# Talking-heads attention and a gated MLP in one kernel: more buffers for scores, and operand differences of the fast matrix products spread over their runs

## The chip, the core and the metric

One core of a Trainium2 chip. The metric is the device time of one launch in microseconds (us), here as the median of three runs. The engines are named as the profile names them: PE (TensorE, matmuls), PEld (its weight loads), DVE (VectorE), ACT (ScalarE), POOL (GpSimd) and SP (SyncE, which issues every DMA of this kernel on one queue).

## The reference, cut to what matters

```
scores = scale * q @ k^T                      # (4 batches, 12 heads, 448, 448)
scores = einsum('bhij,hg->bgij', scores, w_pre)
attn   = exp(scores - max);  attn /= sum + 1e-9
attn   = einsum('bhij,hg->bgij', attn, w_post)
x      = (attn @ v) as (1792 tokens, 768)
h      = x @ w_in                             # w_in 768 x 2048, float64 in memory
out    = (h * sigmoid(h)) @ w_out             # w_out 2048 x 768, float64 in memory
```

## The kernel before, in words

**Attention.** Each of 4 batches is cut into 4 tiles of 110 or 120 query rows; a tile is 11 or 12 groups of ten rows times twelve heads (120 partitions), 180 groups in all. The loop over `groups` writes out one order for all engines. In iteration i, PE mixes group i+3 over the heads (`mix`, L318), DVE takes its maximum (`top`, L324), ACT its exponential (`exp`, L329), POOL scales the second mixing weights by the row sums (`norm`, L337, tile `wr`), and PE mixes group i again (`mix_again`, L344). In between stand pieces of work that `put` has spread over the groups: `scores` (L265) multiplies q and k of the next tile for two heads, ACT copies the two results to `st` tiles (L283), and SP moves each into the grouped layout `g` (L284); `values` (L287) multiplies the mixed weights with v, ACT and DVE bring the two halves together in `xb`, and after every second head SP stores `xb` to `x_dram` (L306). The `st` tiles rotate through 3 buffers of pool `s`, the `wr` tiles through 3.

**Weights.** `convert` turns the MLP's float64 weights into float32 in jobs of two parts, a part in three steps: DVE L86, ACT L90, DVE L92 and L93, then in `finish` DVE L63 and POOL L66. After a job's second part POOL makes sums of the four quarter blocks (L68 to L71), and SP stores seven planes to DRAM (L57). 34 of the 48 jobs run inside attention, the other 14 beside the first matrix product.

**MLP.** Both matrix products are done by a fast scheme with seven multiplications instead of eight on 2 x 2 blocks. The tokens fall into two units u of two batches each. I call one pass of a multiplication for both units a run. The first matrix product (kind "i") has 7 runs of 16 products (products 0 to 111 of list `steps`), each product being 9 matmuls; the second (kind "o") has 7 runs of 6 products (112 to 153) of 24 matmuls. Each float32 operand is split in two float32r halves: `halve` is an ACT cast (L537) and a DVE subtraction (L539). A run's operands are either blocks of x (or of the activated hidden values) or differences of blocks: `differ` (DVE L543, POOL L545) and `second` (DVE L550, ACT L552, POOL L553, DVE L555). `put_at` spreads such items over the products ahead of the run that needs them. In each product of the main loop the order is: matmuls, `ready_part` (ACT cast L520 and POOL subtraction L521 of 256 KB of weights, tiles `wh` and `wl`, `WB` = 7 buffers each), `load_part` (L515), `evacuate` of the product before (DVE or ACT), `put_out` for finished outputs (PE transposes L756, ACT L757, SP L758), then the operand items, then one chunk of `load_x` (SP L481, POOL L476) and one step of `convert`. Product results rotate through four PSUM banks. Unit 0's x is loaded inside attention through two buffers `xr`; unit 1's after attention, one chunk per product.

Of the kernel before, what the change touches and what calls it, by code (L numbers as in the profile page):

```python
# [37 lines left out]
def convert(nc, pool, ebias, jobs):  # L38
# [15 lines left out]
    def store():  # L54
        while made:
            dst, g = made.pop(0)
            nc.sync.dma_start(out=dst, in_=g)  # L57

    def finish(k, pair, g, e):
        n, i = parts[k]  # L60
        lo, hi = pair[:, :, :, 0], pair[:, :, :, 1]
        m = lo.bitcast(F32)
        nc.vector.scalar_tensor_tensor(  # L63
            out=m, in0=lo.bitcast(U32), scalar=(1 if i else -1) * 2.0 ** -32, in1=hi,
            op0=ALU.mult, op1=ALU.add if i else ALU.subtract)
        nc.gpsimd.tensor_mul(out=e, in0=m, in1=e)  # L66
        if not i:
            nc.gpsimd.tensor_add(out=g[:, 4], in0=g[:, 0], in1=g[:, 1])  # L68
            nc.gpsimd.tensor_add(
                out=g[:, 5:7], in0=g[:, 0:5:4], in1=g[:, 2:3].to_broadcast([128, 2, 128]))  # L70
            nc.gpsimd.tensor_add(out=g[:, 0], in0=g[:, 6], in1=g[:, 3])  # L71
            made.append((jobs[n][1], g))

    before = None
    for k in range(len(parts)):
# [4 lines left out]
        if k % 2 == 0:  # L80
            g = pool.tile([128, 7, 128], F32, name="cg", tag="cg", bufs=2)
# [22 lines left out]
def talking_heads_then_silu_mlp(  # L104
# [16 lines left out]
    R = 10  # L121
# [41 lines left out]
    s_p = pool("s", 3, late, side="right")  # L163
# [18 lines left out]
    def load_weights():  # L182

        wrep = e_p.tile([GP, 2, H], F32, name="wrep", tag="wr", bufs=3)
# [3 lines left out]
        blk = e_p.tile([GP, R], F32, name="blk", tag="wr", bufs=3)  # L188
# [98 lines left out]
    def values(n, h):  # L287
# [8 lines left out]
        if h % 2 == 0:  # L296
            xbs[n] = s_p.tile([128, 2, TQ], F32, name="xb", tag="xb" if n + 1 < len(seq) or h % 4 else "s", bufs=2 if n + 1 < len(seq) or h % 4 else 3)
# [5 lines left out]
        def add():  # L303
            nc.vector.tensor_add(out=xb[:, h % 2, :m], in0=po[:, m:2 * m], in1=xb[:, h % 2, :m])  # L304
            if h % 2:
                nc.sync.dma_start(  # L306
                    out=x_dram[b].rearrange("(h p) t -> p h t", p=128)[:, h - 1:h + 1, t0:t0 + m], in_=xb[:, :, :m])
        return [(take, add)]

    class Group:  # L310
# [21 lines left out]
        def norm(self):  # L332
# [3 lines left out]
            self.wr = e_p.tile([GP, GP], F32, name="wr", tag="wr", bufs=3)  # L336
# [22 lines left out]
    kns, vns, qns, ks, vs, qs, gs, ats, xbs = {}, {}, {}, {}, {}, {}, {}, {}, {}  # L359
    jobs = [(wi_src[:, f, c], wi_dram[:, :, f * HC + c, :]) for f in range(HF) for c in range(HC)]  # L360
# [105 lines left out]
    ORDER = (2, 3, 6, 5, 1, 4, 0)  # L466
# [3 lines left out]
    def load_x(u, blocks, lag):  # L470

        chunks = [(j, l, c) for j, l in blocks for c in range(HC)]
        for n in range(len(chunks) + lag):
            if n >= lag:
                r = box["xr"][(n - lag) % 2]
                nc.gpsimd.tensor_add(out=xs[u][chunks[n - lag]], in0=r[:, 0], in1=r[:, 1])  # L476
            if n < len(chunks):
                j, l, c = chunks[n]
                r = box["xr"][n % 2]
# [16 lines left out]
    WB = NP + 1  # L496
# [9 lines left out]

    high_at[3].append(NP)
# [33 lines left out]
    def differ(blocks, c):  # L541

        nc.vector.tensor_sub(out=blocks[0, 0, c], in0=blocks[0, 1, c], in1=blocks[0, 0, c])  # L543
        yield
        nc.gpsimd.tensor_sub(out=blocks[0, 1, c], in0=blocks[1, 1, c], in1=blocks[0, 1, c])  # L545

    def second(blocks, c, dst):

        t = box["t"].tile([128, T], F32, name="t2", tag="t2", bufs=3)
        nc.vector.tensor_sub(out=t, in0=blocks[1, 1, c], in1=blocks[0, 0, c])  # L550
        yield
        nc.scalar.copy(out=dst[:, 0], in_=t)  # L552
        nc.gpsimd.tensor_sub(out=blocks[1, 0, c], in0=t, in1=blocks[1, 0, c])  # L553
        yield
        nc.vector.tensor_sub(out=dst[:, 1], in0=t, in1=raw(dst[:, 0]))  # L555
# [9 lines left out]
    SOURCE = [(0, 0), (1, 0), None, (0, 1), (1, 0), (0, 0), (1, 1)]  # L565
    for kind, n, nk, blocks in (("i", HF, HC, xs), ("o", HC, HF, gr)):
        for m in range(7):
            for u in range(NU):
                s = step_of[kind, m, u, 0]
                if m == 2:  # L570
                    todo = [lambda b=blocks, c=c, u=u: second(b[u], c, ops[u][c]) for c in range(nk)]
                else:
                    todo = [lambda b=blocks, c=c, u=u, at=SOURCE[m]: halve(b[u][(*at, c)], ops[u][c]) for c in range(nk)]
                if kind == "i" and u and not m:
                    put_at(s - n + 3, n - 3, todo)
                elif m or u:
# [3 lines left out]
                if m == 1:  # L580
                    put_at(s, n, [lambda b=blocks, c=c, u=u: differ(b[u], c) for c in range(nk)])
# [3 lines left out]
    later, done, scaled = [], [], False  # L585
    for i in range(len(groups) + 1):
        g, new, old = at(i), at(i + 3), at(i - 1)
        if i == n_last:
# [9 lines left out]
            def xpairs(p, u):  # L598
                xp = {(j, c): pair(p, f"x{u}{j}{c}", F32) for j in range(2) for c in range(HC)}
                xs[u] = {(j, l, c): xp[j, c][:, l] for j in range(2) for l in range(2) for c in range(HC)}  # L600
# [5 lines left out]
            x_next = load_x(0, ((0, 0), (1, 0), (0, 1), (1, 1)), 2)  # L606
# [19 lines left out]
        for _, take in later:  # L626
            if take:
                take()
        if at(i + 2):
# [39 lines left out]
    for h in range(H):  # L669
# [4 lines left out]
        for takes in later:  # L674
            for take in takes:
                if take:
                    take()
        later = [new]
    for take in later[0]:
        take()  # L680
    for n, p in enumerate(phs):
# [13 lines left out]
    box["t"] = pool("t", 1)  # L695
    c2_p = ctx.enter_context(ExitStack())
    conv = convert(nc, pool("c2", 1, c2_p), ebias, jobs[NA:])
    for x in x_next:
        pass
    x_next = load_x(1, ((0, 0), (1, 0), (0, 1), (1, 1)), 2)  # L700
# [6 lines left out]
    def evacuate(s, p):  # L707
# [3 lines left out]
        if kind == "i":  # L711
            U, V = gr[u][0, 1, a], gr[u][1, 1, a]
# [115 lines left out]
```

## Time and profile before

| | us |
|---|---|
| median of 3 runs | 1082.99 (1082.1 to 1087.95) |
| the profiled execution | 1082.58 |
| its span | 1080.9 |
| PE busy | 976.7 (90%) |
| DVE busy | 737.8 (68%) |
| ACT busy | 593.9 (55%) |
| POOL busy | 474.5 (44%) |

The span is what the trace shows from the first to the last instruction. Attention takes about the first 600 us of it and the MLP the rest; the matmuls of product 0 begin at 590, those of the second matrix product at 839. A share of busy time is a mean over such stages, so the rows below are cut by stage.

### The profile page before, as it was taken

What the parts mean: (1) busy time and instruction counts of PE and PEld (TensorE: products, weight loads), DVE (VectorE), ACT (ScalarE), POOL (GpSimd) and SP (SyncE); (2) the same over time, 40 slices, a digit from 0 to 9 for tenths busy, and PEclk for the clock granted to TensorE, in tenths of its full rate; (3) what the DMA queues carried; (4) which work ended last, traced back from release to release, by engine and by line L of the source; (5) the groups of instructions that cost most, each with busy time, mean ns of one, the idle gap of its engine ahead of it and who ended that gap; (6) DMA issues with size and microseconds to landing.
All of it is one profiled execution on the core that took longest, in us unless ns stands there. A gap on an engine that the chain in (4) does not pass through costs nothing.

```text
span 1080.9 us, 17390 instructions
## 1 busy us (share of the span) xinstructions
PE 976.7 (90%) x5448; PEld 787.8 (73%) x5448; DVE 737.8 (68%) x1708; ACT 593.9 (55%) x1450; POOL 474.5 (44%) x605
## 2 busy tenths in 40 slices
PE   6889899898899989989996778899999996999998
PEld 3456666676667766767775757699999994899997
DVE  2578767885778767777884128998886499954442
ACT  4667667775667766767764324433555522432442
POOL 0354323542235423344454547875542379722220
PEclk9899999998999999999998988999999997899999
DMA  6566666667567666576547675354531112211332
GB/s 170 158 182 176 164 181 175 180 184 191 145 169 205 193 164 175 159 205 189 173 125 213 166 185 149 112 158 150 151 103 49 49 48 65 57 49 49 92 101 59
DMA packets 200031, 153.18 MB, mean 142 GB/s; under 512 B 77732, under 2 KB 189188, under 8 KB 199940
## 3 DMA queue, kind: packets, MB, share of 16 engines
q1 hardware_dynamic: 199940, 152.08, 50.1%
q8 instruction: 43, 0.70, 0.3%
q14 instruction: 48, 0.39, 0.1%
HBM read 74.75 MB, written 38.58 MB: 105 GB/s over the span
## 4 chain that ended last, share of the span: by engine, by line
PE 43%; DVE 21%; DMA 20%; ACT 8%; issue 5%; SPq 2%; POOL 2%; ACTq 0%; POOLq 0%; DVEq 0%
DMA g<-st 13%; PE ph L532 10%; PE ph L531 10%; PE ph L533 10%; PE pa L344 5%; DVE nm L324 3%; PE pp L318 3%; DMA xr<-x_dram 3%; PE pqk L278 3%; ACT st L283 3%; DVE at L356 3%; DVE t L550 2%; ACT e L329 2%; DVE cg L92 1%; PE po L293 1%
## 5 line engine op out<-in xcount | busy, mean ns | idle before, releaser
L337 POOL TENSOR_SCALAR wr<-wpost,r 120x120 f32<-120x120 f32 x180 | 83.7, 465 | 330.9 <-DVE r L335 231.3
L344 PE MATMUL pa<-wr,e 120*112 120x120 f32 x1440 | 191.3, 277 | 19.0 <-DVE r L334 16.5
L344 PEld LDWEIGHTS pa<-wr,e 120*112 120x112 f32 x1440 | 165.6, 181 | 48.0 <-issue 24.7
L531 PE MATMUL ph<-op,wh 128*128 128x448 f32 x483 | 183.5, 380 | 11.6 <-ACT g L729 6.0
L532 PE MATMUL ph<-op,wh 128*128 128x448 f32 x483 | 180.8, 374 | 8.1 <-DVE op L539 6.8
L293 PE MATMUL po<-at,v 112*128 112x220 f32 (+1 forms) x768 | 174.4, 355 | 7.2 <-DVE xb L304 2.8
L533 PE MATMUL ph<-op,wl 128*128 128x448 f32 x483 | 180.0, 373 | 0.1
L318 PE MATMUL pp<-g,wpre 120*120 120x448 f32 x360 | 171.9, 562 | 7.8 <-DMA g<-st 4.8
L521 POOL TENSOR_TENSOR wl<-wl,wh 128x512 fp32r<-128x512 f32 x84 | 116.4, 1396 | 133.5 <-ACT wh L520 133.3
L324 DVE TENSOR_REDUCE nm<-pp 120x1 f32<-120x448 f32 x180 | 111.2, 618 | 87.4 <-PE pp L318 87.0
L293 PEld LDWEIGHTS po<-at,v 112*128 112x128 f32 x768 | 116.2, 197 | 73.6 <-issue 52.3
L329 ACT ACTIVATE e<-pp,nm 120x448 f32<-120x448 f32 x180 | 114.8, 638 | 61.5 <-DVE nm L324 60.7
L353 ACT CAST at<-pa 112x480 fp32r<-112x480 f32 x180 | 103.1, 573 | 56.6 <-PE pa L344 56.0
L283 ACT COPY st<-pqk 110x448 f32<-110x448 f32 (+1 forms) x192 | 98.7, 541 | 53.8 <-DMA g<-st 47.9
L356 DVE TENSOR_TENSOR at<-pa,at 112x480 fp32r<-112x480 f32 x180 | 116.5, 647 | 4.7 <-ACT at L353 4.7
L531 PEld LDWEIGHTS ph<-op,wh 128*128 128x128 f32 x483 | 93.0, 193 | 24.4 <-ACT g L729 7.7
L532 PEld LDWEIGHTS ph<-op,wh 128*128 128x128 f32 x483 | 93.2, 193 | 17.3 <-DVE op L539 7.9
L533 PEld LDWEIGHTS ph<-op,wl 128*128 128x128 f32 x483 | 93.1, 193 | 8.7 <-POOL wl L521 0.8
L278 PE MATMUL pqk<-kh,qh 64*110 64x448 f32 (+1 forms) x192 | 65.5, 461 | 27.7 <-ACT st L283 11.5
L66 POOL TENSOR_TENSOR cg<-cw,cg 128x256 f32<-128x256 f32 x96 | 71.5, 745 | 42.7 <-DVE cw L63 42.7
L304 DVE TENSOR_TENSOR xb<-po,xb 128x110 f32<-128x110 f32 (+1 forms) x192 | 50.2, 268 | 51.8 <-ACT xb L301 51.5
L520 ACT CAST wh<-wl 128x512 fp32r<-128x512 f32 x84 | 51.0, 617 | 42.0 <-DMA wl<-wi_dram 22.4
(112 smaller groups left out, 1717.6 us busy)
## 6 DMA issues: line engine op xcount, KB each, us to landing
g<-st SPq DMA_DIRECT2D x144, 192.5 KB
cw<-in_moe_w_in SPq DMA_DIRECT2D x48, 256.0 KB
cw<-in_moe_w_out SPq DMA_DIRECT2D x48, 256.0 KB
wi_dram<-cg SPq DMA_DIRECT2D x24, 448.0 KB
wo_dram<-cg SPq DMA_DIRECT2D x24, 448.0 KB
xr<-x_dram SPq DMA_DIRECT2D x48, 224.0 KB
wl<-wi_dram SPq DMA_DIRECT2D x42, 256.0 KB
wl<-wo_dram SPq DMA_DIRECT2D x42, 256.0 KB
```

Source lines behind the costliest of these rows:

```text
L283: nc.scalar.copy(out=st[:m], in_=ps[i][:m, :S])
L293: nc.tensor.matmul(po[:, :2 * m].rearrange("p (w t) -> p w t", w=2), lhsT=vs[b, h][:, j].rearrange("p a d -> p (a d)"), rhs=ats[n][:, j, h ...
L318: nc.tensor.matmul(self.p[:GP, :S], lhsT=wpre.rearrange("p i g -> p (i g)"), rhs=gs[self.n][:, self.slot, :], start=True, stop=True)
L324: nc.vector.tensor_reduce(out=self.nm, in_=self.p[:GP, :S], axis=AX.X, op=ALU.max, negate=True)
L329: nc.scalar.activation(out=self.e, in_=self.p[:GP, :S], func=AF.Exp, bias=self.nm, scale=1.0, accum_out=self.s)
L344: nc.tensor.matmul(self.pa[:JT, j * GP:(j + 1) * GP], lhsT=self.e[:, j * JT:(j + 1) * JT], rhs=self.wr, start=True, stop=True)
L353: nc.scalar.copy(out=self.hi, in_=self.src)
L356: nc.vector.tensor_sub(out=self.lo, in0=self.src, in1=raw(self.hi))
L521: nc.gpsimd.tensor_sub(out=wl, in0=raw(wl), in1=raw(wh))
L531: nc.tensor.matmul(p[:, :T], lhsT=wh, rhs=x[:, 0], start=(n == 0), stop=False)
L532: nc.tensor.matmul(p[:, :T], lhsT=wh, rhs=x[:, 1], start=False, stop=False)
L533: nc.tensor.matmul(p[:, :T], lhsT=wl, rhs=x[:, 0], start=False, stop=(n == nk - 1))
```

## The change

It has these parts. Pool `s` gets 4 buffers, `wr` 4. The stores of `xb` go into a list and are issued after the iteration's score transfers. `convert` makes its three sums in a tile `ct` of its own (one buffer) with four POOL adds of 128 columns in place of three adds, one of them 256 wide, and stores four planes and three planes by two DMAs.

The seven multiplications come in another order, with other block sums. All operands are blocks; the four differences (`DIFFER`) each lie in one run, with their columns going to DVE and POOL in turn. `evacuate` changes with it: run 2 writes minus the result by ACT, run 3 adds a DVE subtraction and a POOL addition, run 6 makes two DVE additions and two outputs.

The x tiles pair both units, and attention's end loads the first halves (`l` = 0) of both units; the second halves come after attention through five buffers. `WB` falls from 7 to 6. The last 14 conversion jobs begin at product 18 and not 3. `put_out` comes ahead of `evacuate`, with 2 `ob` buffers and not 3.

```diff
-            nc.gpsimd.tensor_add(out=g[:, 4], in0=g[:, 0], in1=g[:, 1])
-            nc.gpsimd.tensor_add(
-                out=g[:, 5:7], in0=g[:, 0:5:4], in1=g[:, 2:3].to_broadcast([128, 2, 128]))
-            nc.gpsimd.tensor_add(out=g[:, 0], in0=g[:, 6], in1=g[:, 3])
-            made.append((jobs[n][1], g))
+            t = pool.tile([128, 3, 128], F32, name="ct", tag="ct", bufs=1)
+            nc.gpsimd.tensor_add(out=t[:, 0], in0=g[:, 0], in1=g[:, 1])
+            nc.gpsimd.tensor_add(out=t[:, 1], in0=g[:, 0], in1=g[:, 2])
+            nc.gpsimd.tensor_add(out=t[:, 2], in0=t[:, 0], in1=g[:, 2])
+            nc.gpsimd.tensor_add(out=g[:, 0], in0=t[:, 2], in1=g[:, 3])
+            made.append((jobs[n][1], g, t))
...
-    s_p = pool("s", 3, late, side="right")
+    s_p = pool("s", 4, late, side="right")
...
-                nc.sync.dma_start(
-                    out=x_dram[b].rearrange("(h p) t -> p h t", p=128)[:, h - 1:h + 1, t0:t0 + m], in_=xb[:, :, :m])
+                stores.append(lambda: nc.sync.dma_start(
+                    out=x_dram[b].rearrange("(h p) t -> p h t", p=128)[:, h - 1:h + 1, t0:t0 + m], in_=xb[:, :, :m]))
...
-    WB = NP + 1
+    WB = NP
+    CONV = 18
...
+    def subtract(eng, out, a, b):
+
+        eng.tensor_sub(out=out, in0=a, in1=b)
         yield
...
+    SOURCE = [(0, 0), (1, 0), (1, 1), (1, 1), (0, 1), (1, 0), (0, 0)]
+    DIFFER = [((0, 0), (0, 1), (0, 0)), ((0, 1), (1, 1), (0, 1)), ((1, 1), (1, 1), (0, 0)), ((1, 0), (1, 1), (1, 0))]
...
+        for d, (x, y, z) in enumerate(DIFFER):
+            for u in range(NU):
+                s = step_of[kind, d, u, 0] if kind == "o" or d > 1 else step_of[kind, 1, d, 0]
+                put_at(s, n - 1 if kind == "i" else n, [
+                    lambda b=blocks, c=c, u=u, x=x, y=y, z=z: subtract(
+                        (nc.vector, nc.gpsimd)[c % 2], b[u][(*x, c)], b[u][(*y, c)], b[u][(*z, c)]) for c in range(nk)])
...
-    x_next = load_x(1, ((0, 0), (1, 0), (0, 1), (1, 1)), 2)
+    x2_p = pool("x2", 1, c2_p)
+    box["xr"] = box["xr"] + [pair(x2_p, f"xs{c}", F32) for c in range(3)]
+    x_next = load_x([(u, j, 1, c) for j in range(2) for u in range(NU) for c in range(HC)])
...
         elif k == 2:
+            nc.scalar.mul(V, p, -1.0)
+        elif k == 3:
             nc.vector.tensor_sub(out=U, in0=p, in1=M)
-        elif k == 3:
-            nc.vector.tensor_sub(out=V, in0=U, in1=p)
+            nc.gpsimd.tensor_add(out=V, in0=V, in1=U)
...
-            t = target(0, 1)
-            nc.vector.tensor_sub(out=t, in0=U, in1=p)
-            finish(t, 0, 1, 1.0)
+            for (i, l), x in (((1, 1), U), ((0, 1), V)):
+                t = target(i, l)
+                nc.vector.tensor_add(out=t, in0=p, in1=x)
+                finish(t, i, l, 1.0)
...
-        ob = box["o"].tile([JT, NJ, 128], F32, name="ob", tag="ob", bufs=3)
+        ob = box["o"].tile([JT, NJ, 128], F32, name="ob", tag="ob", bufs=2)
```

SP's queue after attention, before the change. `xr` are the two load buffers, `x_dram_69` and `x_dram_70` unit 1's batches, `cw` the float64 weights, `wl` the MLP's weights for run 1:

```order
L481 DMA xr_7540<-x_dram_70 64x2x448 x2
L481 DMA xr_7541<-x_dram_70 64x2x448 x2
L515 DMA wl<-wi_dram 128x512
L481 DMA xr_7540<-x_dram_70 64x2x448 x2
L47 DMA cw<-in_moe_w_out 128x2x256
L515 DMA wl<-wi_dram 128x512
```

The same place after the change:

```order
L486 DMA xs_8209<-x_dram_70 64x2x448 x2
L519 DMA wl<-wi_dram 128x512
L486 DMA xr_7642<-x_dram_70 64x2x448 x2
L519 DMA wl<-wi_dram 128x512
L486 DMA xr_7643<-x_dram_70 64x2x448 x2
L519 DMA wl<-wi_dram 128x512 x4
L47 DMA cw<-in_moe_w_out 128x2x256 x4
```

The x loads now rotate through five buffers, and the conversion's loads stand behind all of them and behind run 1's weights.

POOL in run 3 of the first matrix product, before (L521 splits weights, L66 to L71 are the conversion):

```order
L66 TENSOR_TENSOR cg<-cw,cg 128x256
L68 TENSOR_TENSOR cg<-cg 128x128
L69 TENSOR_TENSOR cg<-cg 128x256
L71 TENSOR_TENSOR cg<-cg 128x128
L521 TENSOR_TENSOR wl<-wl,wh 128x512 x2
```

After, where `g_8146` and its like are hidden blocks to which run 3's results are added:

```order
L743 TENSOR_TENSOR g_8146<-g_8146,g_8162 128x448
L743 TENSOR_TENSOR g_8147<-g_8147,g_8163 128x448
L67 TENSOR_TENSOR cg<-cw,cg 128x256
L743 TENSOR_TENSOR g_8148<-g_8148,g_8164 128x448
L743 TENSOR_TENSOR g_8149<-g_8149,g_8165 128x448
L743 TENSOR_TENSOR g_8150<-g_8150,g_8166 128x448
L67 TENSOR_TENSOR cg<-cw,cg 128x256
```

Sixteen additions of 448 columns are new between the conversion's and the weights' instructions.

DVE ahead of run 2 of the second matrix product, before (L543 and L550 are differences, L555 the split's subtraction, L732 evacuates):

```order
L543 TENSOR_TENSOR g_8084<-g_8076,g_8084 128x448
L543 TENSOR_TENSOR g_8085<-g_8077,g_8085 128x448
L543 TENSOR_TENSOR g_8086<-g_8078,g_8086 128x448
L550 TENSOR_TENSOR t_10521<-g_8063,g_8055 128x448
L550 TENSOR_TENSOR t_10526<-g_8064,g_8056 128x448
L550 TENSOR_TENSOR t_10528<-g_8065,g_8057 128x448
L555 TENSOR_TENSOR x_9923<-t_10521,x_9923 128x448
L732 TENSOR_TENSOR oT<-ph,x_8036 128x448
```

After (L547 differences, L543 the split's subtraction, L737 evacuates):

```order
L547 TENSOR_TENSOR g_8173<-g_8189,g_8173 128x448
L543 TENSOR_TENSOR op_7641<-g_8162,op_7641 128x448
L547 TENSOR_TENSOR g_8175<-g_8191,g_8175 128x448
L737 TENSOR_TENSOR oT<-ph,x_7633 128x448
L543 TENSOR_TENSOR x_10058<-g_8163,x_10058 128x448
L543 TENSOR_TENSOR x_10059<-g_8164,x_10059 128x448
L543 TENSOR_TENSOR x_10060<-g_8165,x_10060 128x448
L547 TENSOR_TENSOR g_8177<-g_8193,g_8177 128x448
```

Before, nine subtractions stand between two of run 1's evacuations here, now three to five; every second difference has gone to POOL's queue.

## Rows read from the trace of the kernel before

**Rows 1.** Windows: PE, PEld, DVE, ACT, POOL busy, PEclk, DMA, GB/s.

```profile
27.00:566.00 539.00, 494.71 (x3100) 360.72 (x3100) 395.80 (x1182) 375.12 (x1008) 215.47 (x367) 0.97 0.62 175
621.40:722.60 101.20, 83.92 (x360) 70.90 (x361) 76.66 (x117) 37.80 (x75) 68.64 (x68) 0.92 0.54 154
722.60:752.00 29.40, 29.40 (x146) 27.24 (x146) 25.27 (x44) 9.81 (x20) 19.33 (x22) 1.00 0.50 149
899.40:950.10 50.70, 38.48 (x155) 31.27 (x154) 48.37 (x46) 19.44 (x37) 41.80 (x28) 0.80 0.19 52
```

**Rows 2.** Waits in attention, 27 to 566: us in total, times, longest.

```profile
ACT st L283 <- DMA g<-st: 46.6, 46, 3.0
...
PE pqk L278 <- ACT st L283: 11.5, 11, 2.8
...
PE pqk L278 <- DVE r L334: 6.6, 14, 0.7
```

**Rows 3.** Timeline of ACT, then PE, around 254: start, us, idle before.

```profile
254.47 0.53 ACT L283 COPY st<-pqk 110x448 f32<-110x448 f32 x1 [2.97 <-DMA g<-st]
...
255.06 0.45 PE L278 MATMUL pqk<-kh,qh 64*110 64x448 f32 x1 [2.80 <-ACT st L283]
```

**Rows 4.** Chain of work that ended last, 100 to 200: start, us, what.

```profile
102.12 3.33 DMA g<-st
```

**Rows 5.** Waits in 621.4 to 722.6.

```profile
PE ph L531 <- ACT g L729: 6.0, 4, 2.7
PE ph L532 <- DVE op L539: 5.3, 1, 5.3
...
ACT wh L520 <- DMA wl<-wi_dram: 16.1, 6, 7.7
```

**Rows 6.** Page, DMA issues: number, KB of each.

```profile
xr<-x_dram SPq DMA_DIRECT2D x48, 224.0 KB
```

**Rows 7.** Timeline of DVE and POOL: single instructions with nothing beside them.

```profile
628.28 0.30 DVE L93 TENSOR_SCALAR cw<-cw 128x256 int32<-128x256 int32 x1
...
629.25 0.29 DVE L86 TENSOR_SCALAR cg<-cw 128x256 int32<-128x256 int32 x1
629.45 0.42 DVE L63 SCALAR_TENSOR_TENSOR cw<-cw 128x256 f32<-128x256 uint32 x1
630.04 0.62 DVE L539 TENSOR_TENSOR op<-x,op 128x448 fp32r<-128x448 f32 x1 [0.17 <-ACT op L537]
630.59 0.42 DVE L92 SCALAR_TENSOR_TENSOR cg<-cw,cg 128x256 int32<-128x256 int32 x1
...
571.04 1.13 POOL L476 TENSOR_TENSOR x<-xr 128x448 f32<-128x448 f32 x1 [4.31 <-DMA xr<-x_dram]
...
584.26 1.27 POOL L521 TENSOR_TENSOR wl<-wl,wh 128x512 fp32r<-128x512 f32 x1 [0.25 <-ACT wh L520]
...
644.05 0.74 POOL L66 TENSOR_TENSOR cg<-cw,cg 128x256 f32<-128x256 f32 x1
644.75 0.45 POOL L68 TENSOR_TENSOR cg<-cg 128x128 f32<-128x128 f32 x1
```

**Rows 8.** The same view, where a POOL and a DVE instruction meet.

```profile
637.41 1.16 POOL L476 TENSOR_TENSOR x<-xr 128x448 f32<-128x448 f32 x1 [2.72 <-DMA xr<-x_dram]
...
637.67 1.38 DVE L539 TENSOR_TENSOR op<-x,op 128x448 fp32r<-128x448 f32 x1 [1.16 <-ACT op L537]
```

**Rows 9.** Groups of instructions by line, 899.4 to 950.1: busy, mean ns.

```profile
L550 DVE TENSOR_TENSOR t<-g,g 128x448 f32<-128x448 f32 x13 | 16.8, 1330 | 0.0
L521 POOL TENSOR_TENSOR wl<-wl,wh 128x512 fp32r<-128x512 f32 x10 | 15.4, 1547 | 5.3 <-ACT wh L520 5.2
...
L735 DVE TENSOR_TENSOR x<-ph,x 128x448 f32<-128x448 f32 x5 | 3.1, 614 | 0.2 <-PE ph L533 0.2
```

**Rows 10.** Timeline of PE, then ACT, at the end of the span.

```profile
1074.38 1.04 PE L756 MATMUL ptt<-ident,oT 128*112 128x128 f32 x8
...
1076.50 0.60 ACT L757 ACTIVATE ob<-ptt 112x512 f32<-112x512 f32 x1 [0.34 <-ACT ob L757]
```

## What the change should do to the time

> **What bounds the kernel now.** I read the busy windows by stage first, to see where PE, the busiest engine, stands still; then the waits of each such stage; then single instructions, to price what the change moves.
>
> In products 48 to 63 of the first matrix product PE never stops: 146 matmuls in 29.4 us, 0.201 us each [rows 1]. So a product of nine costs 1.81 us and sixteen cost 29.0. Three stages fall short of that. (a) From 621.4 to 722.6, products 8 to 47, 360 matmuls took 101.2 us; at 0.201 they are 72.5, so 28.7 are lost. (b) From 899.4 to 950.1, run 2 of the second matrix product, 144 product matmuls (the others are transposes) took 50.7 where 29.0 would do: 21.7 lost. DVE is busy for 48.4 of these 50.7, POOL for 41.8, and the granted clock averages 0.80, so part of the stretch ran at 1.2 and not 2.4 GHz. (c) In attention PE is busy 494.7 of 539.0, so 44.3 are open [rows 1].
>
> The waits name the causes. In (a) PE stood behind unit 1's first operands (5.3 once) and behind ACT's evacuations (6.0), which queue behind weight casts that waited 16.1 us for their loads [rows 5]. In (b) DVE does 13 differences of 1330 ns, with their splits beside them [rows 9]. In (c) ACT waited 46.6 us, 46 times, for an `st` buffer whose transfer had not landed, and PE 11.5 us for ACT behind it [rows 2]; one such place shows ACT 2.97 and PE 2.80 us idle [rows 3].
>
> **What DVE and POOL can do together.** Alone, a 448-column subtraction takes DVE 0.62 us and POOL 1.13, a weight split POOL 1.27; a conversion part takes DVE 0.29 + 0.42 + 0.30 + 0.42 = 1.43 and POOL 0.74, and 128 columns take POOL 0.45 [rows 7]. A DVE subtraction that began 0.26 us after a POOL addition took 1.38: it ended 0.48 after POOL did [rows 8]. So the two queue for something. DVE's instructions on PSUM results keep their 614 ns even in (b) [rows 9]. In (b), DVE ran 46 instructions, 7 of them on PSUM, and POOL 28, 10 of them weight splits: undisturbed, 39 x 0.62 + 18 x 1.13 + 10 x 1.27 = 57 us, done in 50.7. I take 1.12 us of such work per us as the pair's limit.
>
> The Trainium skill's page "SBUF — State Buffer", section "Who interferes with whom", speaks against this change: a DVE instruction with two SBUF inputs and a GpSimd instruction that reads SBUF use one read port, held exclusively for a whole instruction. The trace agrees in the meeting above, and disagrees in letter by the 1.12. By its letter, handing every second difference to GpSimd frees no port time; what that would give is the second rival below.
>
> **The change part by part.**
>
> Attention. With four `st` buffers a pair of heads waits for the pair before the last. A transfer's wait was 3.33 us in one place of the chain [rows 4], and a group takes about 3 (some 540 us for 180), so two pairs in a row no longer collide and nearly all of the 46.6 goes. On the path lie PE's 11.5, some of the 6.6 that follow behind DVE [rows 2], and the half clock after the gaps: a mean of 0.97 is 6% of 539 at 1.2 GHz, which costs up to 16 us, a third of which I give to these gaps. All of it would be 20; little may come if DVE (395.8 busy) is late next, so the low end is 3. I take 12, nearer the waits of PE itself. Stores behind transfers take SP's waits away from the transfers, which the fourth buffer mostly hides already: 0, with its worth inside 3 to 20. The fourth `wr` buffer: 0. Conversion gains 0.18 us of POOL (4 x 0.45 for 3 adds) and one DMA per job: 34 jobs, 6 us of POOL, hidden since POOL is busy 215 of 539. The `ct` buffer is written half a job, about 7 us, after its store is asked for, against 3 to 5 us to land: 0.
>
> Products 8 to 15. Unit 1's first operands come with attention's loads, so (a)'s wait for them goes. The loads in attention keep their number and both buffers: 0 there.
>
> Run 1's weights. The second halves of x are 24 transfers of 224 KB [rows 6], 5.5 MB; at attention's 175 GB/s [rows 1], 31 us; from product 2 to 16 pass 14 x 1.81 = 25. With five buffers they run without pause, and the weights asked for between them land up to 6 us late, or not at all late at the 194 GB/s and over that windows near there show. I take 3.
>
> Pair load in the first matrix product. A conversion job (two parts, six products) is 2 x (1.43 + 0.74) + 1.8 = 6.1 us, so sixteen products carry 16.3; six weight splits 7.6; six operand splits 3.7. That is 27.6 of 29.0, and such stretches lose nothing now (products 48 to 63). After: run 1 has conversion from product 18 on (13), the 11.3, twelve differences, eight on DVE and four on POOL (9.5), and the last x adds (1.5): 35, or 31.5 at 1.12 per us. Run 2: 27.6 + six differences 4.7 = 32.3, or 28.8. Run 3: the same plus sixteen POOL additions of run 3's results, 18.1: 50.4, or 45. Excess over 29.0: 2.5 + 0 + 16. DVE may lag about 2.5 products, 4.5 us, before the four PSUM banks stop PE, so 14 are lost; ends 4 (POOL alone late: the additions' targets are not read until run 6) and 21 (no lag allowed).
>
> Run 6 has two DVE additions of 0.61 per product: in eight products 9.8, with 3.8 of conversion and 1.8 of splits in the first half, 5 of the next matrix product's splits in the second: over 15 of 14.5 each, more where POOL meets it, less the lag: 2 lost (0 to 5).
>
> So (a) and what follows lose 3 + 14 + 2 = 19 where 28.7 were lost: 9.7 gained.
>
> Second matrix product. Differences now lie in runs 0 to 3, eight on DVE and eight on POOL in each: 5.0 + 9.0, sixteen splits 9.9, weight splits 7.6: 31.5, or 28 of 29.0 at 1.12. Run 3 has six POOL additions more: 38, or 34, 5 over, less the lag. With run 6's lag carried in I leave 3 (0 to 9): 18.7 gained.
>
> The tail. The last `ob` of three is done 2.7 us after PE's last product now, at 1077.1 against 1074.4 [rows 10]. After, six outputs remain there, for two buffers: ACT fills two (until 1.8 after), then waits about 3.3 (nearest row: `st`'s landing [rows 4]) for each next pair: 4.6 to 5.8, 8.4 to 9.6. That is up to 7 later; I take 6.5 (2 if only ACT's work counts).
>
> Sum against the profiled execution, 1082.58: 12 + 9.7 + 18.7 - 6.5 = 34 less, 1048.7. That execution lies 0.4 under the median, so **1049**.
>
> **The rivals.** The pair's limit is softer: POOL's additions in run 3 fall behind without holding the weights' splits up. For it: nobody reads them for 32 products. Against: POOL is one queue, and splits stand behind the additions. It gives 10 back: 1039.
>
> The port is exclusive to the letter, 1.0 us per us. Then runs 1 to 3 are 35 + 32.3 + 50.4 - 87 = 31 over, less 4.5, 13 more than forecast; the second matrix product 2.5 over in each of runs 0 to 2 and 9 in run 3, 9 more than forecast: 1071. The overlap in (b) speaks against it.
>
> Attention gains 3, since DVE stands where ACT stood: 1058.
>
> Slower: six weight buffers. A part's load can be asked for only after PE's last use, six products (10.9 us) before its next use in the first product, two (9.8) in the second. Asking, landing (3.3), cast and split (1.3) need about 5.5, so it decides once POOL's or SP's queue runs some 5 us behind at a run's end; 8 behind costs 2.6 at each of 13 run changes and eats the whole gain; 9 behind costs 4 at each, 52: 1101. Against it: products 48 to 63 lose nothing at their run change with DVE at 25.3 and POOL at 19.3 of 29.4 [rows 1].
>
> The early inputs are not early, since x's loads are late in attention too, and all else balances: 1083.
>
> **How the numbers follow.** Forecast 42%, softer limit 25%, attention 13%, port to the letter 12%, slower 5%, nothing 3%; other small mixes lie among these. The range from 1030 (softer limit, attention near its upper end) to 1072 (the letter) leaves out the slower case, no change, and the ends of the rest, some 2 in 10. A measurement of this kernel can tell about 0.5%, 5.4 us: faster 0.92, same 0.03, slower 0.05.
>
> **What would show it.** ACT's wait of `st` for `g<-st` near zero, and PE busy over 505 of attention's window. No wait at product 8; casts waiting under 6 us at run 1. DVE and POOL both near full in run 3 of the first product, which takes about 40 us; if it takes 30, the softer limit holds. Run 2 of the second product near 30 us with DVE at four fifths. ACT waiting for `ob` in the last 12 us. The forecast is wrong if run 1 and 2 stretch as run 3 does, or if attention stays.

## The result, and the profile after

The changed kernel takes **1031.2 us** (median of 1029.1 to 1037.19), against 1083 before: a ratio of 0.952, 95% interval 0.947 to 0.957. The forecast was 1049 with a range from 1030 to 1072. So the sign and the range hold, and the gain is 52 us where 34 were forecast. The profiled execution took 1030.98, its span 1029.3.

The busy windows of the changed kernel, with the columns of [rows 1]: attention (the same matmuls but two as in the first of [rows 1]), products 8 to 47, run 3, run 4 of the first matrix product, run 2 of the second.

```profile
27.00:540.00 513.00, 479.06 (x3098) 352.02 (x3099) 391.08 (x1181) 373.12 (x1007) 219.17 (x401) 0.99 0.65 184
597.90:674.80 76.90, 74.63 (x361) 67.08 (x360) 54.98 (x83) 40.99 (x81) 56.12 (x55) 1.00 0.59 162
674.80:705.50 30.70, 29.63 (x145) 26.79 (x144) 29.46 (x39) 8.14 (x16) 29.17 (x29) 1.00 0.35 103
705.50:743.90 38.40, 31.54 (x145) 27.93 (x146) 30.89 (x51) 10.52 (x20) 30.91 (x33) 0.96 0.45 132
862.30:893.20 30.90, 30.36 (x155) 27.78 (x153) 25.59 (x28) 16.98 (x34) 24.73 (x17) 1.00 0.29 82
```

Read beside [rows 1], attention's 3100 matmuls took 539.0 us before and 513.0 now. Products 8 to 47 fell from 101.2 to 76.9, run 2 of the second matrix product from 50.7 to 30.9, with a granted clock of 1.00 there and not 0.80. Worse became above all run 4 of the first matrix product: 38.4, with PE busy for 31.5, where it took 29.2 before. Run 3 went from 29.2 to 30.7, and products 0 to 7 from 31.8 to 33.7.

By the start of the first matmul of a product, read off PE's timeline of both kernels:

| stretch | before | after | gained | forecast |
|---|---|---|---|---|
| to product 0 (attention) | 589.69 | 564.22 | 25.5 | 12 |
| products 0 to 111 | 249.67 | 238.01 | 11.7 | 9.7 |
| products 112 to 152 | 230.06 | 209.52 | 20.5 | 18.7 |
| product 153 to the end | 11.43 | 17.51 | -6.1 | -6.5 |

Three of the four terms came within 2 us. The gain exceeds the forecast's by 17.7 us, and 13.5 of these lie in attention.

Attention's waits of ACT (total, times, longest), to be held against [rows 2]:

```profile
ACT xb L303 <- DMA x_dram<-xb: 16.4, 9, 3.3
ACT st L285 <- DMA g<-st: 4.5, 2, 2.7
```

The wait for scores' transfers fell from 46.6 to 4.5, as forecast. A new one stands above it, which the kernel before does not have in this window: ACT waits for an `xb` buffer whose store has not landed. One such place in ACT's timeline:

```profile
109.48 0.25 ACT L303 COPY xb<-po 128x110 f32<-128x110 f32 x1 [2.95 <-DMA x_dram<-xb]
```

Waits around run 4's start, 700 to 730:

```profile
PEld ph L537 <- POOL wl L525: 8.2, 3, 3.7
PE ph L537 <- POOL wl L525: 6.8, 3, 3.4
```

POOL's timeline at the same place:

```profile
699.27 4.16 POOL L743 TENSOR_TENSOR g<-g,g 128x448 f32<-128x448 f32 x3
703.39 1.33 POOL L547 TENSOR_TENSOR x<-x,x 128x448 f32<-128x448 f32 x1
704.68 0.80 POOL L67 TENSOR_TENSOR cg<-cw,cg 128x256 f32<-128x256 f32 x1
705.44 2.65 POOL L743 TENSOR_TENSOR g<-g,g 128x448 f32<-128x448 f32 x2
708.05 1.45 POOL L525 TENSOR_TENSOR wl<-wl,wh 128x512 fp32r<-128x512 f32 x1
709.46 1.33 POOL L743 TENSOR_TENSOR g<-g,g 128x448 f32<-128x448 f32 x1
```

POOL has no idle time in any of these rows (none carries a bracket). The additions of run 3's results (L743) stand ahead of the splits of run 4's weights (L525), and PE, at product 64 since 705.5, waits for the one that begins at 708.05.

DVE's differences in run 2 of the second matrix product (busy, mean ns), against the thirteen of [rows 9]:

```profile
L547 DVE TENSOR_TENSOR g<-g,g 128x448 f32<-128x448 f32 x9 | 9.8, 1084 | 0.0
```

ACT's last instructions: two `ob` buffers, six outputs.

```profile
1020.65 0.60 ACT L761 ACTIVATE ob<-ptt 112x512 f32<-112x512 f32 x1 [2.19 <-DMA out<-ob]
1021.47 0.60 ACT L761 ACTIVATE ob<-ptt 112x512 f32<-112x512 f32 x1 [0.22 <-DMA out<-ob]
1023.89 0.60 ACT L761 ACTIVATE ob<-ptt 112x512 f32<-112x512 f32 x1 [1.83 <-DMA out<-ob]
1024.99 0.60 ACT L761 ACTIVATE ob<-ptt 112x512 f32<-112x512 f32 x1 [0.50 <-DMA out<-ob]
```

### The profile page after: what moved, and what is told of

Same layout as the page of the kernel before. It is cut to its first block, busy times and chain, and to the rows that moved or that the text cites. A ratio compares the mean times of both kernels' runs of the same rounds, so it can differ in the third digit from the quotient of the medians.

```text
span 1029.3 us, 17594 instructions
## 1 busy us (share of the span) xinstructions
PE 949.2 (92%) x5448; PEld 775.5 (75%) x5448; DVE 734.2 (71%) x1690; ACT 602.1 (59%) x1472; POOL 514.8 (50%) x671
## 4 chain that ended last, share of the span: by engine, by line
PE 57%; DVE 14%; DMA 14%; ACT 5%; POOL 5%; issue 4%; SPq 2%; ACTq 0%; POOLq 0%; DVEq 0%
PE ph L537 10%; PE ph L536 10%; PE ph L535 10%; PE pa L346 9%; PE pp L320 7%; PE pqk L280 6%; DMA x_dram<-xb 4%; PE po L295 4%; DMA g<-st 3%; DVE nm L326 3%; DVE at L358 3%; DMA xs<-x_dram 1%; POOL wl L525 1%; DVE xb L306 1%; ACT st L285 1%
## 5 line engine op out<-in xcount | busy, mean ns | idle before, releaser
L346 PE MATMUL pa<-wr,e 120*112 120x120 f32 x1440 | 188.0, 274 | 19.7 <-DVE r L336 14.2
L346 PEld LDWEIGHTS pa<-wr,e 120*112 120x112 f32 x1440 | 163.2, 179 | 46.8 <-issue 25.8
L535 PE MATMUL ph<-op,wh 128*128 128x448 f32 x483 | 179.2, 371 | 0.4 <-ACT g L734 0.2
L536 PE MATMUL ph<-op,wh 128*128 128x448 f32 x483 | 177.6, 368 | 1.9 <-DVE op L543 1.9
L320 PE MATMUL pp<-g,wpre 120*120 120x448 f32 x360 | 168.8, 552 | 6.8 <-DMA g<-st 5.9
L525 POOL TENSOR_TENSOR wl<-wl,wh 128x512 fp32r<-128x512 f32 x84 | 122.5, 1473 | 84.5 <-ACT wh L524 78.0
L285 ACT COPY st<-pqk 110x448 f32<-110x448 f32 (+1 forms) x192 | 93.9, 546 | 10.8 <-DMA g<-st 6.8
L536 PEld LDWEIGHTS ph<-op,wh 128*128 128x128 f32 x483 | 91.5, 189 | 9.7 <-DVE op L543 2.7
L535 PEld LDWEIGHTS ph<-op,wh 128*128 128x128 f32 x483 | 91.3, 189 | 8.4 <-ACT g L734 0.9
L67 POOL TENSOR_TENSOR cg<-cw,cg 128x256 f32<-128x256 f32 x96 | 74.3, 774 | 42.1 <-DVE cw L64 42.1
L303 ACT COPY xb<-po 128x110 f32<-128x110 f32 (+1 forms) x192 | 48.7, 260 | 53.9 <-DMA x_dram<-xb 36.7
```

The lines of the kernel that those rows point to most:

```text
L285: nc.scalar.copy(out=st[:m], in_=ps[i][:m, :S])
L320: nc.tensor.matmul(self.p[:GP, :S], lhsT=wpre.rearrange("p i g -> p (i g)"), rhs=gs[self.n][:, self.slot, :], start=True, stop=True)
L346: nc.tensor.matmul(self.pa[:JT, j * GP:(j + 1) * GP], lhsT=self.e[:, j * JT:(j + 1) * JT], rhs=self.wr, start=True, stop=True)
L525: nc.gpsimd.tensor_sub(out=wl, in0=raw(wl), in1=raw(wh))
L535: nc.tensor.matmul(p[:, :T], lhsT=wh, rhs=x[:, 0], start=(n == 0), stop=False)
L536: nc.tensor.matmul(p[:, :T], lhsT=wh, rhs=x[:, 1], start=False, stop=False)
```

## Experiments on attention: which of its parts gained twice the forecast?

Theory: the fourth `st` buffer gains it all, and the deferred stores nothing. Rival: the deferred stores, since SP no longer stands before DVE's `xb` while transfers wait behind. Three kernels undo the one, the other, and both. Beside the experiments the kernel before took 1085 to 1091, so times taken at different occasions can differ by some us, and most readings below go by stretches of the profiles.

**Three buffers again (a_s3).**

```diff
-    s_p = pool("s", 4, late, side="right")
+    s_p = pool("s", 3, late, side="right")
```

> The changed kernel with 3 buffers in pool s again (the deferred stores stay). In the changed kernel product 0 begins at 564.2 us of the span, in the kernel before at 589.7. If the fourth buffer is what attention gained by, product 0 begins at 586 to 590 here and ACT's waits of st for g<-st are back at some 45 us; time about 1053 to 1056. If the deferred stores are (SP no longer stands before DVE's xb while transfers wait behind), product 0 begins at 566 to 570, time about 1034 to 1036. If each does half, 575 to 580 and about 1044.

Product 0 began at 591.2, a little later than expected, and the time was 1061.2. The waits are back:

```profile
ACT st L285 <- DMA g<-st: 40.9, 42, 3.0
```

**Stores at once (a_nodefer).**

```diff
-                stores.append(lambda: nc.sync.dma_start(
+                nc.sync.dma_start(
```

> The changed kernel with the stores of xb issued at once, as before; four buffers stay. If the fourth buffer alone brings the gain, product 0 begins at 564 to 567 and the time is about 1031 to 1034. If the deferral brings it, product 0 begins at 585 to 590 and SP stands some 90 us before DVE's xb again; time about 1053. If each does half, 575 to 580.

Product 0 began at 555.6, earlier than in the changed kernel, and the time was 1024.1. No theory had that: the deferral does not merely gain nothing, it costs.

**Both undone (a_s3nd).**

> The changed kernel with both undone: 3 buffers and stores at once. All theories that put the gain of attention into these two parts expect product 0 at 588 to 591 and a time of about 1056. If it begins below 580, the smaller pieces (fourth wr buffer, conversion's POOL additions, loads at attention's end) have a share. If gaps cost half clock, PE's busy time for the same matmuls is about 15 us above the changed kernel's 479 here, beside 10 us more of idle time.

Product 0 began at 589.1, the time was 1055.3. The small pieces (`wr`, conversion, loads at attention's end) have no share that shows. From 27 us to product 0 PE was busy for 515.3, against 495.7 in the changed kernel: 19.6 more, where about 15 were expected, and it was idle for 5.3 more and not 10. Half the clock was granted for 50.0 us against 17.8, so at most 16 of the 19.6 are the clock's.

**The fourth buffer alone, in the kernel before (b_ct4w6).** For the room it takes two parts of the change along: the conversion's sums in `ct`, and six weight buffers.

```diff
-    s_p = pool("s", 3, late, side="right")
+    s_p = pool("s", 4, late, side="right")
...
-    WB = NP + 1
+    WB = NP
```

> The kernel before with the fourth buffer in pool s alone, and the two parts of the change that make room for it: the conversion's sums in a tile of their own, and six weight buffers in place of seven. Stores of xb at once, as before. If the fourth buffer alone brings attention's gain, product 0 begins at 555 to 560 (589.7 before), as in the changed kernel with stores at once. If the change's order of loads at attention's end has a share, 562 to 575. After product 0 the kernel before takes 491 us. If six weight buffers cost nothing, it takes 490 to 494 here, and the time is about 1050. If they cost 2.6 to 4 us at each of 13 run changes (the rival of the prediction that is slower), it takes 525 to 543 and the time is 1083 to 1100.

Product 0 began at 555.1, the time was 1045.0. After product 0 it took 487.1 against 491.2 before, so six weight buffers cost nothing in sum, and the slower rival falls. The window from 27 us to product 0, in the kernel before and then here:

```profile
27.00:589.70 562.70, 510.75 (x3196) 374.15 (x3196) 406.63 (x1214) 384.89 (x1035) 225.09 (x379) 0.97 0.63 177
```

```profile
27.00:555.10 528.10, 496.04 (x3196) 368.18 (x3196) 402.71 (x1216) 384.73 (x1038) 229.77 (x415) 0.98 0.67 189
```

For the same 3196 matmuls the window is 34.6 shorter. PE's idle time fell from 52.0 to 32.1, by 19.9, and its busy time by 14.7. In this pair little of the 14.7 is the clock: half the clock was granted for 33.6 us before and for 26.3 here, and 7.3 us less of that are worth 3.7 at most. Busy time falls at full clock too, as one stretch of both kernels shows, again with the kernel before first:

```profile
189.00:243.00 54.00, 49.75 (x314) 36.19 (x312) 43.77 (x128) 39.90 (x108) 28.28 (x44) 1.00 0.64 182
```

```profile
189.00:243.00 54.00, 53.35 (x358) 39.93 (x357) 41.52 (x126) 42.33 (x114) 22.96 (x43) 1.00 0.68 192
```

That is 0.158 us of busy time for a matmul against 0.149. A matmul that starts behind a gap counts as busy for 0.42 us in the mean, one that starts while another is still running adds 0.15 at full clock. Before, 92 of them start behind a gap, here 50. An estimate from these numbers gives 42 x 0.27 = 11 us, the rest of the 14.7.

**Why the deferral costs (a_xb3).** Theory: with the stores behind the transfers, `xb`'s two buffers come free later. In six profiles with deferred stores ACT's wait for them is 16.4 to 27.2 us, in four with stores at once 8.3 to 10.1. This kernel keeps the deferral and gives `xb` a third buffer, at the price of a slower start.

```diff
-  tag="xb" ..., bufs=2 if n + 1 < len(seq) or h % 4 else 4)
+  tag="xb" ..., bufs=3 if n + 1 < len(seq) or h % 4 else 4)
...
-    nat = pool("nat", 3, early_p)
+    nat = pool("nat", 2, early_p)
```

> The changed kernel, stores of xb still behind the scores' transfers, with three xb buffers and not two; for the room, the loads at the start of the kernel (pool nat) go through two buffers and not three, which may lengthen the first 30 us by some us. With two buffers product 0 begins at 563.2 to 569.4 with the stores behind, and at 554.1 to 557.1 with the stores at once. If the stores behind cost these 9 to 10 us because xb's two buffers come free late (ACT's waits of xb for x_dram<-xb are 16 to 27 us against 9), product 0 begins at 554 to 558 here, some us more if the start is longer, PE's idle time from 27 us to product 0 falls from 38 to 45 to under 37, and the waits of xb for its store nearly vanish. If the cost lies elsewhere (stores in bursts beside the loads of q, k and v), it stays at 563 to 570 with 38 us or more idle.

Product 0 began at 560.5, outside both expected ranges, the time was 1027.6, and the waits of `xb` for its store are gone from the list of waits. The slower start has to be taken out, and the 180 maxima of the groups do that: the first and the last start stand in each row. The kernel before:

```profile
L324 DVE TENSOR_REDUCE nm<-pp x180: 604/617/627, 31.0 to 580.6; 120x1 f32<-120x448 f32 x180
```

The changed kernel:

```profile
L326 DVE TENSOR_REDUCE nm<-pp x180: 602/620/629, 32.1 to 554.7; 120x1 f32<-120x448 f32 x180
```

With stores at once (a_nodefer):

```profile
L326 DVE TENSOR_REDUCE nm<-pp x180: 604/624/630, 31.7 to 548.4; 120x1 f32<-120x448 f32 x180
```

With the third `xb` buffer (a_xb3):

```profile
L326 DVE TENSOR_REDUCE nm<-pp x180: 606/624/627, 36.0 to 548.1; 120x1 f32<-120x448 f32 x180
```

The loop over the groups took 549.6 before, 522.6 in the changed kernel, 516.7 with stores at once and 512.1 with the third buffer. The start was 3.9 us later, and 560.5 less 3.9 is 556.6, inside what the buffer theory expected. PE's idle time was to fall under 37 and was 40.6, against 41.5 in the changed kernel. Before 40 us, in the longer start, it was 2.5 higher than there, and without these 2.5 the expectation is still missed. So that `xb`'s buffers are what the deferral costs is borne out by the waits and by the length of the loop, but not proven: two things were changed at once, and the idle time did not follow.

## Experiments on run 3: what makes PE stand at products 64 to 68?

Runs 3 and 4 took 69.0 us, where 58.4 would be without a stop: 10.7 lost. Theory: sixteen POOL additions are too much for run 3. Rivals: the six weight buffers or late loads of weights, and, if it is the additions, whether POOL's queue alone or a limit of both engines counts.

**Without the additions (a_noadd).** The kernel leaves out this step of the computation.

```diff
-            nc.gpsimd.tensor_add(out=V, in0=V, in1=U)
+            if kind == "o":
+                nc.gpsimd.tensor_add(out=V, in0=V, in1=U)
```

> The changed kernel without the sixteen additions into V in run 3 of the first matrix product (this part of the computation is left out). Runs 3 and 4 take 30.7 + 38.3 = 69.0 us in the changed kernel, 58.4 if PE never stops. If the additions alone cause the stop, by POOL's queue or by the pair's limit, the two runs take 58.4 to 60 here: 10 off, time about 1020. If six weight buffers or late weight loads have a part, the waits for wl's splits at products 64, 65 and 68 stay in part: 62 to 69.

Runs 3 and 4 took 29.2 each, what PE needs without a stop; the time was 1021.3. Their windows:

```profile
673.50:702.70 29.20, 29.20 (x145) 27.07 (x145) 25.59 (x45) 10.12 (x20) 19.70 (x25) 1.00 0.46 136
702.70:731.90 29.20, 29.20 (x146) 27.05 (x145) 24.58 (x43) 8.68 (x17) 18.70 (x21) 1.00 0.51 147
```

**All on DVE (a_dve), and every second one on DVE (a_split).**

```diff
-            nc.gpsimd.tensor_add(out=V, in0=V, in1=U)
+            nc.vector.tensor_add(out=V, in0=V, in1=U)
...
+            (nc.gpsimd, nc.vector)[a % 2].tensor_add(out=V, in0=V, in1=U)
```

> The changed kernel with run 3's addition into V on DVE and not on POOL. If POOL's queue is what makes PE stand at products 64, 65 and 68 (10.7 us lost over runs 3 and 4), these waits for wl's splits go; DVE then has 33 us of work for run 3's 29 and lags by 4 to 7, so 0 to 5 come back as waits for operand splits: time 1021 to 1026. If the six weight buffers or late weight loads are the cause, the waits at 64 to 68 stay: 1030 to 1033. If DVE and POOL share one limit of 1.12 us per us and only that counts, run 3 and 4 together lose some 6: 1026.

> The changed kernel with every second addition into V on DVE, the others on POOL. Alone and undisturbed, run 3 then holds some 28.5 us of DVE's work and 28.8 of POOL's for 29.2 of PE. If each engine is bound only by its own work, runs 3 and 4 take 58.4 to 61. If the two share one limit of 1.12 us of work per us, 46.3 of shared work take 41.3, and with the lag that goes free in the changed kernel (16 over, 10.7 lost) some 7 are lost: 65 to 66. With all additions on DVE they took 66.3.

All on DVE, the two runs took 66.3; half and half, 67.3. The first means 8.0 lost, where POOL's queue alone allowed 0 to 5 and the shared limit 6: no theory had it. The times, 1030.1 and 1035.7, cannot be told from the changed kernel's; product 0 began some 5 us later in these two profiles. With the halves, neither engine has 29 us of work by itself, so the theory of own work alone (58.4 to 61) falls; the shared limit (65 to 66) is near, 1 to 2 us too low. The groups by line of the half-and-half kernel over both runs show why:

```profile
L743 POOL TENSOR_TENSOR g<-g,g 128x448 f32<-128x448 f32 x8 | 11.0, 1370 | 3.7 <-DVE g L742 3.7
L743 DVE TENSOR_TENSOR g<-g,g 128x448 f32<-128x448 f32 x8 | 7.6, 947 | 0.3
```

The addition takes 1370 ns on POOL and 947 on DVE, against 1.13 and 0.62 us alone [rows 7]. With all on DVE, PE also waited for DVE's evacuations, and still for a split:

```profile
PE ph L537 <- POOL wl L525: 2.9, 1, 2.9
...
PE ph L535 <- DVE g L742: 2.0, 2, 1.2
```

The Trainium skill's page "SBUF — State Buffer", section "Who interferes with whom", has the port that the two share locked for a whole instruction; the longer means agree that the two wait for each other. In run 2 of the first matrix product the letter, priced by whole durations, does not show: by the prices of [rows 7], the instructions of DVE on SBUF alone and of POOL that began in its 29.3 us add up to some 36 us, 1.2 per us. That is also more than the 1.12 that was taken as the pair's limit, which is thus no constant.

**Additions held back (a_late).** Ten of the sixteen are issued one by one between products 66 and 89. This needs the addend to live on, so run 4's result goes to the free tile. It has stores at once and five output buffers too.

```diff
+            add = lambda: nc.gpsimd.tensor_add(out=V, in0=V, in1=U)
+            if kind == "i" and a >= HC:
+                held.append(add)
+            else:
+                add()
...
-            nc.vector.tensor_sub(out=U, in0=U, in1=p)
+            t = gr[u][1, 0, a] if kind == "i" and a >= HC else U
+            nc.vector.tensor_sub(out=t, in0=U, in1=p)
+            if t is not U:
+                gr[u][1, 0, a], gr[u][1, 1, a] = U, t
...
+        if held and s >= 66 and (s - 66) * 2 // 5 > (s - 67) * 2 // 5:
+            held.pop(0)()
```

> The changed kernel with stores at once and five output buffers in the last run (together 1020.1), and with ten of run 3's sixteen additions into V held back and issued one by one between products 66 and 89; for these the result of run 4 goes to the tile that is still free, so that the addend lives on. Same work in all, six of 16 additions in run 3. If the stop at products 64 to 68 comes of POOL's queue in run 3 being over full, run 3 holds 39.1 us of shared work, 34.9 at 1.12, 5.7 over and about what lags freely: runs 3 and 4 take 58.4 to 60.5 (69.8 in the kernel with these two changes alone), time 1009 to 1012. If it is the pair's total over runs 3 and 4 that counts, 64 to 69 stay and the time is 1015 to 1020.

Runs 3 and 4 took 61.3 (69.8 with the other two changes alone), 0.8 above what the theory of POOL's queue expected, and the time was **1011.3** (1009.6 to 1013.9), a ratio of 0.930, interval 0.926 to 0.935: faster than both kernels. Of the loss of 10.7, 2.9 is left. Five of the ten additions now fall into run 5, so the pair's total over runs 3 and 4 became less too; but by the total 64 at least were expected. What counts more is what stands in POOL's queue ahead of the splits when a run ends. The windows of runs 3 and 4:

```profile
664.20:694.50 30.30, 29.36 (x145) 26.90 (x144) 29.06 (x42) 8.70 (x18) 25.64 (x26) 1.00 0.44 131
694.50:725.40 30.90, 29.98 (x146) 26.98 (x145) 30.44 (x45) 9.67 (x19) 27.01 (x31) 1.00 0.48 141
```

## Experiments on the second matrix product and the tail

**All differences on DVE (a_diffdve).**

```diff
-                        (nc.vector, nc.gpsimd)[c % 2], b[u][(*x, c)], b[u][(*y, c)], b[u][(*z, c)]) for c in range(nk)])
+                        nc.vector, b[u][(*x, c)], b[u][(*y, c)], b[u][(*z, c)]) for c in range(nk)])
```

> The changed kernel with all operand differences on DVE; they stay spread over the runs. Run 2 of the second matrix product took 50.7 us before and 30.97 after. If spreading them is what gains, the second matrix product stays as it is (run 2 at 31, runs 0, 1 and 3 within 0.5), since DVE has 23.5 us of work there for 29, and the pair's work even falls. If handing half of them to POOL is needed, runs 0 to 3 of it stretch by 1 to 5 us each. In the first matrix product run 3 has 1.0 us less of shared work: runs 3 and 4 take 67.5 to 69, the time is 1028 to 1033.

Run 2 of the second matrix product took 30.2, runs 0, 1 and 3 what they took in the changed kernel (29.2, 30.9, 29.2). Runs 3 and 4 of the first took 69.6, over the 67.5 to 69 expected, and the time was 1032.7. The second matrix product has 64 differences in the kernel before and in the changed one, half of them on DVE in both; what differs is which blocks they take and where they stand. So the spreading gains, and handing half to POOL gains nothing here.

**Five output buffers (a_ob5), and with stores at once (a_nd_ob5).**

```diff
+        n = next(count)
+        if last_run and n % 5 > 1:
+            ob = pair(gw, f"x01{n % 5 - 2}", F32)[:JT].rearrange("p l t -> p (l t)")[:, :512].rearrange("p (j c) -> p j c", j=NJ)
+        else:
+            ob = box["o"].tile([JT, NJ, 128], F32, name="ob", tag="ob", bufs=2)
```

> The changed kernel with five output buffers in the last run: the two ob and three dead tiles of x. From product 153's start to the end of the span the changed kernel takes 17.5 us, the kernel before 11.4. If ACT's waits for two ob buffers are what the tail gained (4.7 us of waiting for out<-ob), it takes 13 to 14.5: 3 to 4.5 off, time about 1027. If the transfers of six outputs themselves are the limit (1.4 MB, some 7 us from 1018), it takes 15 to 17.

> The changed kernel with the stores of xb at once (as in the earlier run that took 1024.1) and five output buffers in the last run. If both gains are real and add up, product 0 begins at 555 to 565 and the tail takes 13 to 14.5 us: time 1018 to 1023, below the changed kernel's 1031. If the stores at once gained by a chance of that run only, product 0 begins at 564 to 570 and the time is 1026 to 1031.

From product 153's start to the end it took 14.0 in both, against 17.5. ACT no longer waits for a store:

```profile
1023.88 1.13 ACT L766 ACTIVATE ob<-ptt 112x512 f32<-112x512 f32 x2 [0.35 <-ACT x L766]
1025.31 1.13 ACT L766 ACTIVATE x<-ptt 112x512 f32<-112x512 f32 x2 [0.30 <-PE ptt L765]
```

The first alone took 1033.0: its attention ended at 568.3, late enough to hide 3.5 us. The second took 1020.1 (ratio 0.939, interval 0.933 to 0.945) with product 0 at 557.1, so both gains are real and add up.

## Why the prediction was right, and where it was off

**Attention, forecast 12, measured 25.5: the term that left its bounds of 3 to 20.** The step that failed is the one that weighed what lies on the path: "PE's 11.5, some of the 6.6 that follow behind DVE [rows 2], and the half clock after the gaps", of whose 16 us it took a third. The fourth buffer alone gave 34.6 (product 0 at 555.1): 19.9 of idle time, more than the 18 of those two rows together, and 14.7 of busy time. The third taken for the clock, 5.3, was not too small in that pair: it was 3.7 at most. What the sum put at nothing is the busy time of the matmuls that start behind a gap, some 11 us, and PE's waits in front of other matmuls; before those of the second mixing its idle time fell from 11.3 (27 to 566) to 6.6 (27 to 532 of b_ct4w6). "All of it would be 20" was no upper bound. So the rival by which DVE stands where ACT stood falls too. The second failed step priced the stores behind transfers at "0, with its worth inside 3 to 20": it is below zero. With four `st` and two `xb` buffers, product 0 began at 563.2 to 569.4 in six profiles with deferred stores, at 554.1 to 557.1 in four with stores at once. Some 10 of the fourth buffer's gain were given back. The text priced the deferral by the waits of SP that it takes away from the transfers, and did not ask how long the moved step holds its buffers. That PE would be busy over 505 of attention's window was also wrong, in kind: PE has less busy time when its gaps go.

**What was luck.** The two failed steps of attention offset each other in part: with stores at once, and all else as in the changed kernel, the time was 1024.1, below the range. The range's lower end, 1030, had been set for the softer limit with attention near its upper end, and that limit did not hold. In the first matrix product, 11.7 against 9.7 is a sum of misses too: products 0 to 7 became 1.9 longer, products 8 to 47 gained 24.2 where 25.7 were due, and runs 3 to 6 lost 10.7 and not 16.

**Products 8 to 15.** Unit 1's first operands: the wait at product 8 is gone, 25.0 us became 14.9. Right.

**Run 1's weights, forecast 3.** Products 16 to 31 took 32.7 against 29.2: 3.5 lost. The size was right, the place only in part. PE stood 2.1 us behind POOL's splits, and at the two longest of these places POOL had been busy without a pause, with additions of x and with operand differences. One of them, PE first and then POOL:

```profile
622.86 0.47 PE L537 MATMUL ph<-op,wl 128*128 128x448 f32 x1 [1.02 <-POOL wl L525]
```

```profile
618.92 2.66 POOL L481 TENSOR_TENSOR x<-xr 128x448 f32<-128x448 f32 x2
621.54 2.91 POOL L525 TENSOR_TENSOR wl<-wl,wh 128x512 fp32r<-128x512 f32 x2
```

So late weights and run 1's pair load, whose 2.5 over were to be hidden by the lag, share the 3.5; how was not tried. That casts would wait under 6 us was wrong, 8.1 for products 8 to 47:

```profile
ACT wh L524 <- DMA wl<-wi_dram: 8.1, 3, 5.2
```

**Pair load, forecast 14 in run 3.** 10.7 lost, caused by the additions and nothing else (a_noadd). The place was wrong: run 3 itself took 30.7 and not 40; the debt fell due at run 4's first weight splits. By the text's own test ("if it takes 30, the softer limit holds") the softer limit would have won, and it did not: the splits were held up. The test looked at the run that holds the work, and not at the first one that waits for it. Run 2 did not stretch, and run 1 did by the 3.5 told above. The letter of the port rule, priced by whole durations, falls by the count of run 2: some 36 us of work in 29.3.

**Run 6, forecast 2 lost.** It took 29.2: nothing. **Second matrix product, forecast 18.7 gained.** Run 2 gained 19.8, and of the 3 us left over for runs 0 to 3 hardly anything was needed: PE stood for 0.5 of run 2's 30.9, and the other three took no longer than before. **Tail, forecast 6.5 later.** 6.1, and of these 3.5 go with three more buffers; where the other 2.6 lie was not tried.

## What to carry to other kernels

Price a gap of PE twice: its own length, and the busy time that it adds behind it, by matmuls that start with nothing running ahead of them and by those at the lower clock; here the second was 14.7 us against 19.9. A store that is moved back holds its buffer longer, so ask what waits for that buffer before you defer it. Where an engine's queue is over full, look for the cost at the next consumer of that queue, and move what nobody waits for behind what somebody does.

## What was not expected of the hardware

In some profiles products run a little slower with a granted clock of 1.00: sixteen products of the first matrix product take 29.76 us and not 29.18, with no gap between matmuls. The same window in the changed kernel, then in the last one (a_late):

```profile
740.00:770.00 30.00, 30.00 (x149) 27.80 (x149) 24.08 (x44) 15.41 (x30) 18.32 (x24) 1.00 0.49 143
```

```profile
740.00:770.00 30.00, 30.00 (x147) 27.25 (x146) 28.10 (x51) 20.61 (x41) 21.32 (x26) 1.00 0.46 134
```

147 matmuls where 149 ran; from start to start it is mostly 207 ns and not 203. It comes and goes by execution (in the first matrix product a_ob5 and a_xb3 show it, a_dve and a_noadd don't) and is worth 0.6 us per run. What does it stays open. Open too is why attention ends at 563 to 564 in three profiles with deferred stores and at 568 to 569 in three others.
